# Gated linear attention and a low-rank mixer: two more units loaded raw and turned by VectorE, and another order in the first batch's attention

## The chip, the core and the metric

The kernel runs on one core of a Trainium2 chip. The metric is device microseconds of one execution. The four runs of the kernel before took 502.76 to 505.43 us, with a median of 503.75 us.

## What is computed

All inputs are random. There are 4 batches, 8 heads, 768 steps and 48 channels a head. The mixer works on 384 channels (8 heads of 48), with a rank of 32 and a hidden width of 1536.

```python
f = 1.0 / (1.0 + np.exp(-f_logit))
for t in range(S):                                  # attention, for each batch and head
    state = f[:, :, t, :, None] * state + np.einsum('bhd,bhe->bhde', k[:, :, t], v[:, :, t])
    y[:, :, t] = np.einsum('bhd,bhde->bhe', q[:, :, t], state)
x = y.transpose(0, 2, 1, 3).reshape(B, S, H * D)    # bridge
u = x + (x.transpose(0, 2, 1) @ U @ V).transpose(0, 2, 1)
out = u + np.maximum(u @ w_ch1, 0.0) @ w_ch2        # mixer
```

q, k, v and f_logit are 32-bit floats. The four weights U, V, w_ch1 and w_ch2 come as 64-bit floats, so the kernel makes 32-bit floats of them out of integer operations.

## The kernel before

**Units.** The attention is cut into 16 units: unit n is a pair of heads of batch n // 4. A unit's 768 steps are cut into 12 chunks of 64. In each unit, cumulative products of the gates f are made by scans; the keys k are multiplied by X (the product from a step to its chunk's end) and the queries q by Y (the product from the chunk's start). Then products of 48 or 64 rows give the scores inside a chunk (`sc`), what each chunk adds to the state (`ds`), and the output y out of both.

**Turning the inputs.** f, k and q have to stand with channels on the partitions. There are two ways. For batches 0 and 1 (`b < TURNED`, with TURNED = 2, so units 0 to 7) a tensor is loaded with steps on the partitions (line 394, two DMAs of 128x6x48), and TensorE turns it by six 128x128 transposes into PSUM (`on_tensor`, line 506). ScalarE (f, line 527) or VectorE (k and q, line 518) then read it from PSUM. For batches 2 and 3 (units 8 to 15) it is loaded in blocks of 32 steps (line 400, four DMAs of 32x24x32 or 32x24x16), and VectorE turns every 32x32 block (`turned`, line 483); the multiplication (line 521) then reads SBUF alone.

**The pieces of a unit.** The front of unit n has five: `gates` (f to the sigmoid `fz`), `keep` (scan X, and small operations on it, lines 540 to 550), `keys` (k times X, into `kz`), `read_back` (scan Y, line 558) and `queries` (q times Y, into `qT`). Each tensor's load for unit n + 2 is issued when unit n has read its buffer (`follow`, line 497). The rear has six: `kept` (TensorE turns kz back, line 610, and ScalarE copies it to `kb`, line 614), `states` (ScalarE's copy `whole`, line 618; the products `ds`, line 626; ScalarE's copy `added`, line 632), `scan` (VectorE, line 641, in place in `added`; for batches 1 to 3 ScalarE then copies the result to `st`, line 648), `scores` (line 589, then VectorE's mask A, line 596), `read` (products of q with the state, line 661, and ScalarE's small copy `seen`, line 668) and `inner` (products of A with v, line 679, then ScalarE's copy into the mixer's x, line 685).

**The mixer of a batch.** `low_rank` (line 146), `added_up` (line 154) and `mix` (line 171, with VectorE's addition to x, line 161), then `turn` (line 181), the first channel product `pz` (line 193, with ScalarE's relu, line 200) and the second: plain `po` (line 215) for batch 0, and a form with seven quarter products `pw` (line 238) for the others.

**What sets the order.** TensorE's order is written out by hand for the whole kernel, and so is that of VectorE and ScalarE for the part described here; behind that a scheduler orders VectorE and ScalarE. TensorE, VectorE, ScalarE and the DMA queue of SP each work in order. The stages are:

1. The attention of batch 0 alone, units 0 to 3 (lines 755 to 775). `busy(n)` puts n idle products (128x384, line 753) into TensorE's queue, whose result nobody reads.
2. The start of batch 0's mixer (from line 778), with one idle product ahead of each of its first three pieces, and one weight conversion (lines 64 to 69, on ScalarE, VectorE and GpSimd) put beside each piece but the second and third. From the tenth piece on (EARLY = 9), pieces of batch 1's attention are laid between.
3. The second product of batch 0, laid between the pieces of units 4 to 8 (line 796).
4. Batches 1, 2 and 3 in the same manner, without weight conversions.

**Buffers.** There are two sets of f, k and q buffers, used by even and odd units. In PSUM, a ring of three double banks (`ps_big`) serves pt, sc, ds, y, pu and put, and a ring of two banks (`ps_mm`) serves ph, pz, po and pw. `whole` and `kb` have one buffer each.

## Time and profile before

| | |
|---|---|
| median of 4 runs | 503.75 us (502.76 to 505.43) |
| the profiled execution | 503.66 us, of which the profile's span is 501.9 us |
| busy: TensorE, weight loads | 486.0 us, 405.2 us |
| busy: VectorE, ScalarE, GpSimd | 274.9 us, 157.4 us, 37.6 us |
| transposes of f, k, q on TensorE (line 506) | 144, of which 36 are those of units 6 and 7 |
| transposes on VectorE (line 483) | 24, of 128x768 each |
| idle products (line 753) | 17 (34 records) |
| DMA | 149269 packets, 34.32 MB |

"PE" is TensorE, "PEld" its weight loads, "DVE" VectorE, "ACT" ScalarE, "POOL" GpSimd, and "SPq" the DMA queue of SP. An ordinary 32-bit product leaves two records on PE, so "x6" of `po` is three products; a transpose leaves one. In timeline rows the first number is the start in us, the second the duration, and brackets hold the idle time of that engine ahead of it and what ended it.

### The profile page before, as it was taken

The page shows a single profiled execution, that of the slowest core. Times are in us where ns is not written, and L with a number is a line of the kernel's source. Part 1 is how long each engine was busy: PE and PEld are TensorE (multiplying, and loading weights), DVE is VectorE, ACT ScalarE, POOL GpSimd, SP SyncE. Part 2 cuts the span into 40 slices and gives each one's busy share as a digit, 9 for nine tenths or more (in the row PEclk, how much of TensorE's full clock was granted, in tenths as well). Part 3 has the DMA queues.
Part 4 walks back from the last instruction along what each step waited for, and adds up shares of the span by engine and source line. Part 5 has one row for each costly group of instructions (what it writes and reads, how often), then busy time and mean ns, then how long its engine had stood idle before and what let it go on. Part 6 is the DMA issues. An engine that isn't in the chain of part 4 may idle for free.

```text
span 501.9 us, 12045 instructions
## 1 busy us (share of the span) xinstructions
PE 486.0 (97%) x5319; PEld 405.2 (81%) x5319; DVE 274.9 (55%) x396; ACT 157.4 (31%) x297; POOL 37.6 (7%) x49
## 2 busy tenths in 40 slices
PE   6898999999999999999999999999999999999995
PEld 4666688887666568898898888898899888999995
DVE  5885989777587757656864436632411431222232
ACT  2424665564433313423332222413311122101010
POOL 3001345442000000000000000000000000000000
PEclk9997999999999999999999999999999999999999
DMA  9989977634667422424534100100000000000001
GB/s 145 152 171 230 205 190 173 174 88 62 105 106 112 81 40 29 66 28 88 64 50 80 25 31 3 25 1 34 2 3 31 2 33 1 0 33 0 33 1 39
DMA packets 149269, 34.32 MB, mean 68 GB/s; under 512 B 139798, under 2 KB 147670, under 8 KB 149206
## 3 DMA queue, kind: packets, MB, share of 16 engines
q1 hardware_dynamic: 149206, 33.44, 35.8%
q8 instruction: 44, 0.72, 0.6%
q14 instruction: 19, 0.16, 0.1%
HBM read 28.70 MB, written 4.72 MB: 67 GB/s over the span
## 4 chain that ended last, share of the span: by engine, by line
PE 92%; SPq 3%; DMA 3%; issue 1%; DVE 1%; ACT 0%
PE pz L193 38%; PE pw L238 25%; PE po L215 10%; PE pt L506 3%; PE y L661 3%; PE sc L589 3%; SPq L394 2%; PE y L679 2%; PE ds L626 2%; PE put L181 2%; DMA k_raw<-in_k_dram 1%; PE pt L610 1%; DMA f_raw<-in_f_logit_dram 1%; PE idle L753 1%; PE pu L171 1%; PE ph L146 1%
## 5 line engine op out<-in xcount | busy, mean ns | idle before, releaser
L193 PE MATMUL pz<-uT,w 128*128 128x256 f32 x864 | 195.8, 382 | 0.1
L193 PEld LDWEIGHTS pz<-uT,w 128*128 128x128 f32 x864 | 161.1, 190 | 22.1 <-issue 0.3
L200 ACT ACTIVATE z<-pz 128x512 f32<-128x512 f32 x63 | 37.6, 596 | 131.6 <-PE pz L193 127.5
L238 PE MATMUL pw<-w,z 128*128 128x192 f32 x324 | 56.5, 329 | 0.4 <-DVE o L161 0.4
L238 PE MATMUL pw<-zw,w_raw 128*128 128x192 f32 x324 | 55.9, 327 | 0.0
L238 PEld LDWEIGHTS pw<-w,z 128*128 128x128 f32 x324 | 52.8, 190 | 2.3 <-DVE o L161 1.6
L238 PEld LDWEIGHTS pw<-zw,w_raw 128*128 128x128 f32 x324 | 53.0, 190 | 1.3 <-DVE o L161 1.2
L161 DVE TENSOR_TENSOR w_raw<-z 128x768 f32<-128x768 f32 x18 | 17.2, 954 | 56.3 <-ACT z L200 56.3
L69 POOL TENSOR_TENSOR w<-w_y,w_r 128x384 int32<-128x384 int32 x24 | 31.5, 1311 | 35.9 <-DVE w_y L68 28.0
L540 DVE TENSOR_TENSOR_SCAN X<-fz,ends 128x768 f32<-128x768 f32 x16 | 28.1, 1756 | 10.7 <-ACT fz L527 6.4
L558 DVE TENSOR_TENSOR_SCAN Y<-fz,starts 128x768 f32<-128x768 f32 x16 | 27.9, 1745 | 0.2
L641 DVE TENSOR_TENSOR_SCAN added<-added,whole 128x576 f32<-128x576 f32 x16 | 21.6, 1352 | 9.0 <-ACT added L632 9.0
L215 PE MATMUL po<-w,zw 128*128 128x384 f32 x72 | 25.6, 499 | 0.0
L215 PE MATMUL po<-w,z 128*128 128x384 f32 x72 | 25.3, 495 | 0.0
L161 DVE TENSOR_TENSOR w_y<-x,pw 128x192 f32<-128x192 f32 x9 | 3.2, 354 | 38.5 <-ACT w_y L251 38.5
L596 DVE TENSOR_TENSOR A<-sc,causal 128x768 f32<-128x768 f32 x16 | 15.2, 947 | 16.1 <-PE sc L589 16.1
L648 ACT COPY st<-added 128x576 f32<-128x576 f32 x12 | 14.7, 1223 | 18.9 <-DVE added L641 18.9
L161 DVE TENSOR_TENSOR w_y<-w_y,pw 128x192 f32<-128x192 f32 x18 | 6.2, 347 | 25.6 <-PE pw L238 25.6
L215 PEld LDWEIGHTS po<-w,zw 128*128 128x128 f32 x72 | 12.9, 189 | 8.7 <-issue 1.2
L614 ACT COPY kb<-pt 128x768 f32<-128x768 f32 x16 | 12.8, 798 | 22.4 <-PE pt L610 22.4
L66 DVE TENSOR_SCALAR w_y<-w_y 128x384 f32<-128x384 f32 (+3 forms) x27 | 13.1, 485 | 11.8 <-ACT w_y L64 11.5
L215 PEld LDWEIGHTS po<-w,z 128*128 128x128 f32 x72 | 12.9, 190 | 8.1 <-DVE o L161 0.6
(102 smaller groups left out, 533.0 us busy)
## 6 DMA issues: line engine op xcount, KB each, us to landing
w_raw<-in_moe_w_ch_dram SPq DMA_DIRECT2D x18, 384.0 KB, 3.7
out_dram<-o SPq DMA_DIRECT2D x24, 192.0 KB, 1.9
f_raw<-in_f_logit_dram SPq DMA_DIRECT2D x16, 144.0 KB, 4.5
k_raw<-in_k_dram SPq DMA_DIRECT2D x16, 144.0 KB, 4.1
q_raw<-in_q_dram SPq DMA_DIRECT2D x16, 144.0 KB, 4.2
v_nat<-in_v_dram SPq DMA_DIRECT2D x16, 144.0 KB, 4.4
v_nat<-in_v_dram SPq DMA_DIRECT2D x32, 72.0 KB, 3.0
zw<-in_moe_w_ch_dram SPq DMA_DIRECT2D x6, 384.0 KB, 7.2
```

Source lines behind the costliest of these rows:

```text
L69: nc.gpsimd.tensor_tensor(dst.bitcast(I32), shaped(y.bitcast(I32)), shaped(r), ALU.add)
L161: nc.vector.tensor_tensor(*args)
L193: nc.tensor.matmul(pm[:, i * 2 * P : (i + 1) * 2 * P], lhsT=w1[:, m, o : o + P], rhs=uT[a][:, m, :], start=(m == 0), stop=(m == NDC - 1))
L200: nc.scalar.activation(z[a, c][:, k : k + 2, :].rearrange("p i t -> p (i t)"), pm, AF.Relu)
L215: nc.tensor.matmul(pm, lhsT=z[a, i // NI][:, i % NI, s * P : (s + 1) * P], rhs=w2[:, i, :], start=(i == 0), stop=(i == NFC - 1))
L238: nc.tensor.matmul(pm[:, n * HM : (n + 1) * HM], lhsT=lhs[:, i, :], rhs=rhs[:, i, :], start=(i == 0), stop=(i == NI - 1))
L506: nc.tensor.transpose(pt[:, 2 * c // NBL, c % (NBL // 2) * P : (c % (NBL // 2) + 1) * P], nat[n % 2][nm][:, c].rearrange("p h d -> p (h d) ...
L540: nc.vector.tensor_tensor_scan(backwards(X, S - 1, S), backwards(f, S, S), backwards(ends, S - 1, S), 0.0, ALU.mult, ALU.add,)
L558: nc.vector.tensor_tensor_scan(Y, f[:, 0:S], starts, 0.0, ALU.mult, ALU.add)
L589: nc.tensor.matmul(sc[part[s ^ par], par, c * C : (c + 1) * C], lhsT=T["k"][rows[par], chunk[2 * c + s]], rhs=T["q"][rows[par], chunk[2 * ...
L596: nc.vector.tensor_tensor(T["A"], sc[:, :, 0 : NBL * C].rearrange("p h (c i) -> p h c i", i=C), causal.unsqueeze(1).unsqueeze(1).broadcast ...
L641: nc.vector.tensor_tensor_scan(states, states, T["whole"].rearrange("p e c -> p (e c)"), 0.0, ALU.add, ALU.mult)
```

## The change

- `TURNED` becomes 6 and is compared with the unit, not the batch. Units 6 and 7 are therefore loaded in blocks of 32 and turned by VectorE, as units 8 to 15 are.
- ScalarE's copy `whole` moves from the beginning of `states` to `kept`, ahead of the copy `kb`, for all units.
- The scan of batch 0 writes to a tile of its own (`st`, two buffers) in the layout that it had in `added`. For the other batches the result is the same as before.
- Idle products: one in place of two at the beginning, and none ahead of the mixer's first piece.
- Unit 3 has its `states` ahead of the `read` of unit 2. Its own `read` comes ahead of the first two weight conversions, not after them.
- In batch 0's mixer no weight conversion is put beside the first piece; the one that was there stands beside the third piece.

```diff
-    TURNED = 2
+    TURNED = HP + HP // 2
...
-                if nm == "v" or b < TURNED:
+                if nm == "v" or n < TURNED:
...
         def operand(nm, of):
             t = T[nm] = kz[n % 2][:, C:] if nm == "k" else two.tile([P, S], F32, name="qT")
-            if b < TURNED:
+            if n < TURNED:
                 nc.vector.tensor_tensor(halves(t), on_tensor(nm), halves(T[of]), ALU.mult)
             else:
                 turned(t, r[nm])
...
         def gates():
             f0 = T["f0"] = two.tile([P, NCH], F32, name="f0")
-            if b < TURNED:
+            if n < TURNED:
...
+            whole = T["whole"] = one.tile([P, D, NCH], F32, name="whole")
+            nc.scalar.copy(whole, wholes[n % 2].unsqueeze(1).broadcast_to((P, D, NCH)))
             kb = T["kb"] = one.tile([P, 2, NBL, PAD], F32, name="kb")
             nc.scalar.copy(kb.rearrange("p h c d -> p h (c d)"), pt[:, :, 0 : NBL * PAD])
 
         def states():
-            whole = T["whole"] = one.tile([P, D, NCH], F32, name="whole")
-            nc.scalar.copy(whole, wholes[n % 2].unsqueeze(1).broadcast_to((P, D, NCH)))
...
         def scan():
 
-            states = added[:, 0 : D * NCH]
+            st = T["st"] = two.tile([P, NCH, D], F32, name="st")
+            by_e = "p (e c) -> p c e"
+            if b == 0:
+                states = st.rearrange("p c e -> p (c e)")
+                T["st"] = states.rearrange(by_e, c=NCH)
+            else:
+                states = added[:, 0 : D * NCH]
             with tc.high_priority(offset=AHEAD):
                 nc.vector.tensor_tensor_scan(
-                    states, states, T["whole"].rearrange("p e c -> p (e c)"), 0.0, ALU.add, ALU.mult
+                    states, added[:, 0 : D * NCH], T["whole"].rearrange("p e c -> p (e c)"), 0.0, ALU.add, ALU.mult
                 )
-                T["st"] = states.rearrange("p (e c) -> p c e", c=NCH)
                 if b > 0:
 
-                    st = two.tile([P, NCH, D], F32, name="st")
-                    nc.scalar.copy(st, T["st"])
-                    T["st"] = st
+                    nc.scalar.copy(st, states.rearrange(by_e, c=NCH))
...
-        busy(2)
+        busy(1)
...
-                pieces += rear(n - 1, "read") + rear(n, "states", "scan", "scores") + rear(n - 1, "inner")
+                pieces += rear(n, "states") + rear(n - 1, "read") + rear(n, "scan", "scores") + rear(n - 1, "inner")
...
-        for piece in loads[:2] + rear(HP - 1, "read", "inner") + loads[2 : early + 2]:
+        for piece in rear(HP - 1, "read") + loads[:2] + rear(HP - 1, "inner") + loads[2 : early + 2]:
...
-        idles = {0: 1, 1: 1, 2: 1}
+        idles = {1: 1, 2: 1}
...
-            if loads and i not in (1, 2):
+            if loads and i > 1:
                 loads.pop(0)()
```

## The prediction, made before the changed kernel ran

> **What bounds the kernel now.** I read the page's first two parts, then busy times by stretch, then the timelines of TensorE and VectorE in the stretches that the change touches.

> ```profile
> PE 486.0 (97%) x5319; PEld 405.2 (81%) x5319; DVE 274.9 (55%) x396; ACT 157.4 (31%) x297; POOL 37.6 (7%) x49
> ...
> PEclk9997999999999999999999999999999999999999
> ```

> TensorE is busy for all but 16 us, and its clock is below full in the fourth slice alone (37.6 to 50.2 us). By stretch (length, then busy time of PE, PEld, DVE, ACT, POOL, then clock, DMA share, GB/s):

> ```profile
> 39.80:43.20 3.40, 1.77 (x112) 1.63 (x104) 1.38 (x2) 1.37 (x3) 0.00 (x0) 1.00 1.15 318
> 43.20:46.60 3.40, 2.58 (x103) 2.42 (x96) 1.93 (x5) 1.63 (x6) 0.00 (x0) 0.52 0.83 151
> 46.60:50.10 3.50, 3.50 (x54) 2.01 (x58) 1.99 (x7) 1.95 (x5) 1.19 (x3) 0.50 1.04 166
> ...
> 113.00:140.00 27.00, 27.00 (x455) 18.47 (x457) 17.64 (x22) 10.65 (x20) 3.31 (x2) 1.00 0.59 85
> 140.00:168.00 28.00, 28.00 (x447) 17.50 (x440) 23.29 (x28) 10.84 (x20) 0.00 (x0) 1.00 0.66 104
> ```

> From 57.9 us, where the first `pz` starts, to about 496 us the same table shows less than half a microsecond of idle TensorE. There every microsecond off TensorE shortens the run, if nothing else becomes late. Ahead of 57.9 us the kernel is a chain of waits through DMA, TensorE, ScalarE and VectorE. The two halves are summed apart.

> **Units 6 and 7: what leaves TensorE.** TensorE's timeline where unit 6 is turned (f, then k):

> ```profile
> 112.72 0.82 PE L506 MATMUL pt<-ident,f_raw 128*128 128x128 f32 x6
> 113.38 2.10 PE L215 MATMUL po<-w,z 128*128 128x384 f32 x6
> 115.32 0.82 PE L506 MATMUL pt<-ident,k_raw 128*128 128x128 f32 x6
> 116.06 0.90 PE L661 MATMUL y<-st,qT 48*64 48x48 f32 x44
> ```

> The next group starts 0.66 us after f's six transposes and 0.74 after k's. The durations (0.82, or 0.27 each) overlap, so the pitch from start to start counts. The six groups that go hold 0.66, 0.74, 0.75, 0.71, 0.65 and 0.75: 4.26 us. A `po` group takes 1.94 us ahead of transposes and 2.13 ahead of the small products that now follow some of them. Laying the stretch from 112.72 to 140.36 out again with these pitches gives 23.85 us in place of 27.64: **3.8 us** off TensorE.

> **What VectorE gets.** It keeps the multiplications (0.95 us from PSUM, 0.96 from SBUF) and gets six transposes of 0.97, 5.8 us. VectorE does this already for units 8 and 9:

> ```profile
> 141.37 0.97 DVE L483 STREAM_TRANSPOSE fT<-f_raw 128x768 f32<-128x768 f32 x1
> 143.24 1.76 DVE L540 TENSOR_TENSOR_SCAN X<-fz,ends 128x768 f32<-128x768 f32 x1 [0.90 <-ACT fz L535]
> ...
> 153.46 0.97 DVE L483 STREAM_TRANSPOSE fT<-f_raw 128x768 f32<-128x768 f32 x1
> ```

> One unit takes it 12.1 us, from one fT to the next, including 0.9 us of waiting for ScalarE's sigmoid. TensorE's unit will take 23.85 / 2 = 11.9. So VectorE isn't free cover here: it is level with TensorE, and what counts is its lead. I followed its queue from the last weight conversion (ends at 115.3) with these durations, on the clock of before. kz of unit 6 is ready at 121.4 and TensorE comes to `kept` at 124.4; A of unit 5 is ready at 127.1, wanted at 129.6 (`ds` of unit 6 takes that bank of the ring); kz of unit 7 at 133.9, wanted at 136.5; scores' A of unit 6 at 140.2, wanted at 141.7. None is late. What is late is ScalarE: with six tiles fewer in the ring of three, `kept` of units 6 and 7 takes the bank that its copy of y into x frees, and that copy is queued behind `st`, which waits for VectorE's scan. It ends at 124.7 and 137.2, 0.3 and 0.4 us late (the second with the first counted). GpSimd's last conversion stretches a small VectorE operation at 117.05 to 0.79 us, where the same takes 0.17 at 130.40; a transpose there may lose as much. I take **0.9 us** of waits (0 to 2.5).

> The loads of these units change too: 24 DMAs in place of 12. Four issues hold SP for 2.04 us at 113.61, two for 0.97 at 88.06, so SP gets 6 x 1.07 = 6.4 us more; it is waiting for free weight buffers for 30.5 us in all. The packets double, by 9216. At the page's mean (35.8% of 16 x 501.9 us over 149206 packets, 19 ns) that is 11 us of all engines, where the stretch from 57.9 to 113 leaves 18.7 us of them unused. The weight loads queued behind are wanted four conversions later, some 11 us, and land in 3.7. Zero, with 1 us as the upper end if they slip.

> [...]

> **The start up to 37 us.** One idle product fewer lets f of unit 0 be turned up to 0.64 us earlier (its first weight load is at 4.82, after a wait for issue alone, the transposes at 5.46). That gain ends here:

> ```profile
> 19.92 0.85 PE L506 MATMUL pt<-ident,f_raw 128*128 128x128 f32 x6 [1.13 <-DMA f_raw<-in_f_logit_dram]
> ```

> Unit 2's f lands at 19.79, SP having issued without a pause since 0.8 us. Zero; even a slower start has 1.1 us of slack. From there to 37 us the order of TensorE and VectorE stays. `whole` goes from behind x to ahead of kb, in time in which ScalarE waits for TensorE, and has to wait for the scan of the unit before (17.9 us for unit 1's): kb comes up to 0.7 us later and is wanted 4 us later. Zero. In the later batches the copy is equally covered: ScalarE is 14 to 40% busy.

> **The start from 37 to 58 us.** `ds` of unit 3 ahead of `read` of unit 2 brings its scan forward by 0.8 us, but TensorE then halts for instructions (1.63 us at 40.93 before, ending at 42.56), which ends the scores of unit 3 at 43.2 in both. `seen` of unit 3 no longer stands behind four conversion operations (at 46.09, while `read` ended at 45.73): 0.35 us. The idle product ahead of `low_rank` goes: up to 0.8 us, but h stands behind conversions on ScalarE (51.37 before) and profits by 0.1 to 1.0. The largest piece is on VectorE:

> ```profile
> 54.55 0.56 DVE L68 SCALAR_TENSOR_TENSOR w_y<-zw,w_y 128x384 uint32<-128x384 uint32 x1
> 55.03 2.68 DVE L161 TENSOR_TENSOR x<-x,pu 128x768 f32<-128x768 f32 x3
> ```

> x waits behind the third w1 conversion (53.08 to 55.03), as h's second copy does on ScalarE. Both now go ahead of it. Following the chain (`ph`, h, `ph`, h, `pu`, x, `put`, uT, `pz`), `pz` starts at 56.55 with the clock at half as before and at 55.7 with it full: 1.3 to 2.2 us. The conversion moved is wanted at the second set of `pz`, 7.8 us after the first; it ends by about 59. I take **1.6 us** (-1.2 to 2.2).

> The lower end is the clock. Idle products are there to be busy, and three stretches above show what a gap costs: TensorE busy for 52% of 3.4 us, then 6.7 us at half speed. [...] By the row, a gap of 1.63 us sufficed. If half speed lasts one such stretch longer (to 53.5), the chain loses about 2.8 us against my sum, hence -1.2.

> **The sum.** 503.66 us (span 501.9 and 1.76 around it) - 3.8 + 0.9 - 1.6 = 499.16, so **499.2 us**. The profiled execution is 0.1 us below the median of 503.75.

> **Rivals.**
> - *The start gives nothing, or loses.* The clock stays at half longer, as above, and only the transposes count: 503.66 - 2.9 + 0.5 = 501.3. For it: fewer idle products and waits for h. Against it: the halt in unit 3's scores gets shorter, as `ds` now fills part of it. 16%.
> - *VectorE becomes the bound of units 6 and 7*, without a fall of the clock: waits of 2.5 us in place of 0.9, 500.8. For it: 12.1 us a unit against 11.9. 12%.
> - *Slower: waits for VectorE bring the clock down.* If VectorE or the copy behind it comes 1.3 us later than I have it, `kept` of units 6 and 7 waits 1.6 us each, the gap that sufficed before. Each then costs 1.6 and half of 6.7: 5.0. Two cost 9.9, and the time is 503.66 - 3.8 - 1.6 + 9.9 = 508.2. Against it: at units 8 and 9, with the same 12.1 us, TensorE never waits. 9%.
> - *The start gains more.* The shorter halt leaves the clock at full and `pz` starts at 55.7 or before; VectorE is in time: 503.66 - 3.8 - 2.2 = 497.7. 15%.

> The forecast itself has 48%, from 498 to 500.8.

> A measurement of this kernel can tell about 0.5% from no change, 2.5 us, so "faster" is below 501.2. The forecast and the fuller gain lie there, the second rival for the most part, and the first in a third: 0.76. Within 0.5%: 0.14. Slower: 0.10. The range goes from 497.0 (the fuller gain and some of the start's 20 us) to 502.2 (the first rival with its clock).

> **What will show it.** Line 483 with 30 transposes, the turning on TensorE with 108. First `pz` at 56.3 us or so, not 57.9. The distance from the first `pz` to the last product shorter by about 2.9. No TensorE wait over 0.6 us between 105 and 165. A granted clock of full from 58 us on. Unit 2's f still waited for at 19.8. I am wrong if `kept` waits for ScalarE's x by over a microsecond, if half speed shows behind 53 us or in units 6 and 7, or if a weight comes late to `po`.

## The result and the profile after

| | before | after |
|---|---|---|
| median | 503.49 us (501.53 to 506.36) | 502.1 us (499.88 to 505.27) |
| ratio after / before | | 0.9975, 95% interval 0.9966 to 0.9985 |
| profiled execution (span) | 503.66 us (501.9) | 502.02 us (500.3) |
| first `pz` starts | 57.89 us | 59.07 us |
| first `pz` to the last group of `pw` | 436.33 us | 433.43 us |

The change gains 0.25%, about 1.3 us, where 4.5 were forecast. The last two rows split it: behind the first `pz` the kernel is 2.9 us shorter, ahead of it 1.2 us longer. The page after, busy times and clock:

```profile
PE 482.3 (96%) x5279; PEld 401.2 (80%) x5279; DVE 279.2 (56%) x402; ACT 157.8 (32%) x297; POOL 36.3 (7%) x49
...
PEclk9997899999999999999999999999999999999998
```

TensorE has 3.7 us less to do. The same stretches as before, and one more (columns as there; the clock stands third from the end):

```profile
39.80:43.20 3.40, 0.62 (x31) 0.48 (x28) 1.36 (x1) 0.16 (x1) 0.00 (x0) 1.00 1.08 291
43.20:46.60 3.40, 3.15 (x127) 2.99 (x126) 0.96 (x1) 1.01 (x4) 0.00 (x0) 0.58 0.86 165
46.60:50.10 3.50, 2.42 (x56) 1.82 (x58) 2.50 (x9) 2.22 (x9) 1.04 (x2) 0.50 0.89 169
50.10:53.90 3.80, 3.80 (x15) 1.52 (x8) 3.40 (x7) 1.94 (x5) 1.56 (x3) 0.50 1.13 170
113.00:140.00 27.00, 27.00 (x459) 17.42 (x458) 23.69 (x32) 11.98 (x22) 2.02 (x3) 1.00 0.60 85
140.00:168.00 28.00, 28.00 (x413) 16.82 (x412) 24.73 (x30) 10.62 (x21) 0.00 (x0) 1.00 0.79 123
```

TensorE works for 0.62 us of the first stretch, where it worked for 1.77 before. It is at half speed from 43.8 to 54.0, where it was from 43.3 to 50.1. Between 113 and 168 us it has no idle time, although VectorE is now busy for 88% of it.

**Units 6 and 7.** TensorE's timeline at unit 6's front and at its `kept`:

```profile
114.03 2.10 PE L215 MATMUL po<-w,z 128*128 128x384 f32 x6
116.06 0.90 PE L664 MATMUL y<-st,qT 48*64 48x48 f32 x44
...
124.31 1.45 PE L215 MATMUL po<-w,zw 128*128 128x384 f32 x4
125.70 0.59 PE L610 MATMUL pt<-ident,kz 64*128 64x64 f32 x12
```

No transposes of f and k stand around the `po` group, and `kept` shows no wait. ScalarE's copy of y into x, whose bank it takes, ran from 125.01 to 125.65: it was in time, by 0.05 us. From the first `pz` to the first one of batch 1's mixer it took 127.6 us before and takes 123.8: 3.8 us less.

**The start.** TensorE's timeline before, then after ("issue" is a wait for which the profile shows no releaser):

```profile
42.56 0.74 PE L589 MATMUL sc<-qT,kz 48*64 48x64 f32 x35 [1.63 <-issue]
...
48.00 1.65 PE L753 MATMUL idle<-ends,ident 128*128 128x384 f32 x2
49.58 1.74 PE L146 MATMUL ph<-x,U 128*32 128x384 f32 x12
51.25 0.91 PE L753 MATMUL idle<-ends,ident 128*128 128x384 f32 x2
```

```profile
39.82 0.47 PE L589 MATMUL sc<-qT,kz 48*64 48x64 f32 x11
43.07 0.74 PE L589 MATMUL sc<-qT,kz 48*64 48x64 f32 x34 [2.78 <-issue]
43.59 1.40 PE L682 MATMUL y<-v_nat,A 64*64 64x48 f32 x48
...
49.40 2.77 PE L146 MATMUL ph<-x,U 128*32 128x384 f32 x12 [0.84 <-POOL V L69]
52.10 1.65 PE L756 MATMUL idle<-ends,ident 128*128 128x384 f32 x2
...
59.07 1.10 PE L193 MATMUL pz<-uT,w 128*128 128x256 f32 x4
```

The halt in unit 3's scores, 1.63 us before, is 2.78. It ends at 43.07, where it ended at 42.56. `ph` starts at 49.40, where it started at 49.58: up to here the change is still 0.18 us ahead, since the idle product ahead of `ph` is gone. What it loses, it loses behind it, at half speed: `ph` (1.74 us before) takes 2.77 and the idle product behind it 1.65 (0.91 before).

**A new wait where batch 2's mixer begins.** TensorE, then ScalarE, after:

```profile
279.25 1.48 PE L146 MATMUL ph<-x,U 128*32 128x384 f32 x12
281.52 2.71 PE L238 MATMUL pw<-zw,w_raw 128*128 128x192 f32 x15 [0.79 <-DVE o L161]
```

```profile
279.65 0.83 ACT L535 ACTIVATE fz<-fT 128x756 f32<-128x756 f32 x1 [3.73 <-DVE fT L483]
280.39 0.30 ACT L251 COPY w_y<-pw 128x192 f32<-128x192 f32 x1
```

Before, this place had no wait. The copy of `pw` to w_y can go as soon as `pw` ends at 279.3, but stands behind a sigmoid that waits for VectorE's turn of f. The scheduler now puts that turn behind four additions for `w_raw` (before: behind one), a reordering far behind the edit. VectorE before, then after:

```profile
277.61 0.96 DVE L161 TENSOR_TENSOR w_raw<-z 128x768 f32<-128x768 f32 x1 [3.89 <-ACT z L200]
278.49 0.97 DVE L483 STREAM_TRANSPOSE fT<-f_raw 128x768 f32<-128x768 f32 x1
...
277.77 0.95 DVE L161 TENSOR_TENSOR w_raw<-z,w_raw 128x768 f32<-128x768 f32 x1
278.64 0.97 DVE L483 STREAM_TRANSPOSE fT<-f_raw 128x768 f32<-128x768 f32 x1
```

### The profile page after: what moved, and what is told of

It reads as the page before. It is cut to its first block, busy times and chain, and to the rows that moved or that the text cites. A ratio compares the mean times of both kernels' runs of the same rounds, so it can differ in the third digit from the quotient of the medians.

```text
span 500.3 us, 11989 instructions
## 1 busy us (share of the span) xinstructions
PE 482.3 (96%) x5279; PEld 401.2 (80%) x5279; DVE 279.2 (56%) x402; ACT 157.8 (32%) x297; POOL 36.3 (7%) x49
## 2 busy tenths in 40 slices
DMA packets 158676, 34.30 MB, mean 69 GB/s; under 512 B 149206, under 2 KB 157078, under 8 KB 158614
## 3 DMA queue, kind: packets, MB, share of 16 engines
q1 hardware_dynamic: 158614, 33.44, 36.3%
## 4 chain that ended last, share of the span: by engine, by line
PE 92%; DVE 2%; DMA 2%; SPq 2%; issue 1%; ACT 1%; POOL 0%; DVEq 0%; POOLq 0%; ACTq 0%
PE pz L193 38%; PE pw L238 24%; PE po L215 10%; PE y L664 3%; PE sc L589 3%; PE y L682 2%; PE ds L626 2%; PE pt L506 2%; PE put L181 2%; PE pt L610 1%; PE idle L756 1%; SPq L394 1%; PE ph L146 1%; PE pu L171 1%; DMA f_raw<-in_f_logit_dram 1%
## 5 line engine op out<-in xcount | busy, mean ns | idle before, releaser
L200 ACT ACTIVATE z<-pz 128x512 f32<-128x512 f32 x63 | 37.6, 596 | 129.9 <-PE pz L193 125.8
L161 DVE TENSOR_TENSOR w_raw<-z 128x768 f32<-128x768 f32 x18 | 17.2, 954 | 56.3 <-ACT z L200 56.3
L540 DVE TENSOR_TENSOR_SCAN X<-fz,ends 128x768 f32<-128x768 f32 x16 | 28.1, 1757 | 10.0 <-ACT fz L535 5.1
L69 POOL TENSOR_TENSOR w<-w_y,w_r 128x384 int32<-128x384 int32 x24 | 30.2, 1257 | 36.8 <-DVE w_y L68 32.7
L215 PE MATMUL po<-w,zw 128*128 128x384 f32 x72 | 25.6, 499 | 0.0
L215 PE MATMUL po<-w,z 128*128 128x384 f32 x72 | 25.3, 496 | 0.0
L161 DVE TENSOR_TENSOR w_y<-x,pw 128x192 f32<-128x192 f32 x9 | 3.2, 354 | 38.2 <-ACT w_y L251 38.2
L161 DVE TENSOR_TENSOR w_y<-w_y,pw 128x192 f32<-128x192 f32 x18 | 6.3, 349 | 25.5 <-PE pw L238 25.5
L215 PEld LDWEIGHTS po<-w,zw 128*128 128x128 f32 x72 | 12.9, 189 | 8.7 <-issue 1.2
L215 PEld LDWEIGHTS po<-w,z 128*128 128x128 f32 x72 | 13.1, 190 | 8.5 <-DVE o L161 0.6
L238 PE MATMUL pw<-w,w_raw 128*128 128x192 f32 x108 | 19.2, 328 | 0.0
L682 PEld LDWEIGHTS y<-v_nat,A 64*64 64x64 f32 x768 | 14.0, 144 | 6.1 <-issue 4.8
L238 PEld LDWEIGHTS pw<-w,w_raw 128*128 128x128 f32 x108 | 17.7, 190 | 1.1 <-issue 1.1
```

What stands on the lines that cost most here:

```text
L69: nc.gpsimd.tensor_tensor(dst.bitcast(I32), shaped(y.bitcast(I32)), shaped(r), ALU.add)
L161: nc.vector.tensor_tensor(*args)
L200: nc.scalar.activation(z[a, c][:, k : k + 2, :].rearrange("p i t -> p (i t)"), pm, AF.Relu)
L215: nc.tensor.matmul(pm, lhsT=z[a, i // NI][:, i % NI, s * P : (s + 1) * P], rhs=w2[:, i, :], start=(i == 0), stop=(i == NFC - 1))
L238: nc.tensor.matmul(pm[:, n * HM : (n + 1) * HM], lhsT=lhs[:, i, :], rhs=rhs[:, i, :], start=(i == 0), stop=(i == NI - 1))
L540: nc.vector.tensor_tensor_scan(backwards(X, S - 1, S), backwards(f, S, S), backwards(ends, S - 1, S), 0.0, ALU.mult, ALU.add,)
```

## The experiments

The theory: the transposes give all that was forecast of them, and the start loses it again, because TensorE halts longer for its instructions and its clock stays at half for longer. The rivals: VectorE is late for units 6 and 7 after all; the start loses by its missing idle products, or by the moved conversion. The table's comparisons are with the kernel before on the same chip; single profiles differ among themselves, and where they speak against the medians, the medians count.

| kernel | median us | ratio to before, 95% interval |
|---|---|---|
| e1 transposes alone | 500.21 | 0.9934 [0.9912, 0.9957] |
| e2 start alone | 506.01 | 1.0040 [1.0027, 1.0053] |
| e3 change, idle products back | 501.85 | 0.9955 [0.9938, 0.9971] |
| e4 change, four w1 loads later | 500.75 | 0.9941 [0.9922, 0.9961] |
| e5 transposes, conversion | 500.04 | 0.9934 [0.9915, 0.9953] |
| e6 transposes, order | 502.97 | 0.9978 [0.9962, 0.9995] |
| e7 transposes, fewer idle products | 501.48 | 0.9957 [0.9937, 0.9977] |
| e8 transposes, four w1 loads later | 502.99 | 0.9987 [0.9968, 1.0006] |
| e9 transposes, copy on VectorE | 500.53 | 0.9934 [0.9911, 0.9956] |
| e10 transposes of units 4 and 5 too | 509.86 | 1.0114 [1.0083, 1.0145] |
| e12 transposes, states first | 501.90 | 0.9964 [0.9944, 0.9983] |
| e13 transposes, read first | 500.97 | 0.9941 [0.9921, 0.9961] |
| e14 transposes, conversion, fewer idle products | 500.77 | 0.9944 [0.9923, 0.9965] |
| e15 transposes, order, fewer idle products | 502.41 | 0.9967 [0.9945, 0.9989] |
| e16 e5 with the copy on VectorE | 499.40 | 0.9919 [0.9888, 0.9949] |
| e17 e5 with two w1 loads later | 500.42 | 0.9936 [0.9914, 0.9958] |
| e18 change, six w1 loads later | 505.24 | 1.0028 [1.0008, 1.0048] |
| e19 e5 with four w1 loads later | 499.19 | 0.9907 [0.9886, 0.9927] |

**e1 and e2: each half alone.** e1 is the kernel before with this edit; e2 is the change without it.

```diff
-    TURNED = 2
+    TURNED = HP + HP // 2
...
-            if b < TURNED:
+            if n < TURNED:
```

> The kernel before with units 6 and 7 loaded raw and turned by VectorE, and nothing else of the change. Theory (the transposes give what TensorE's pitches say, and the start takes it back): from the first pz to the end 3.9 us less, so 499.6 us, ratio 0.992; if the scheduler's order of the sigmoid ahead of the copy of pw in batch 2 comes along with it, 0.8 us less of that, 500.4. Rival (the transposes give little, because the stage stands on VectorE or the DMA): 502 us or more, ratio 0.997 or above.

> The changed kernel with units 6 and 7 turned by TensorE as before: all of the change but the transposes. Theory: slower than the kernel before by what the start loses, 1.2 us in the two profiles, 504.7 us, ratio 1.002 to 1.005, and a mean clock below 0.99. Rival (transposes give little): the start is then what makes the change 1.3 us faster, 502.2 us, ratio 0.9975.

The transposes alone gain 3.4 us (500.21 beside 503.64), the start alone loses 2.4 by the medians and 2.0 by the ratio, more than the 1.2 between the two profiles. The sum of both is close to the whole change. e1's page and its timeline at the start:

```profile
PEclk9999999999999999999999999999999999999998
```

```profile
41.87 0.74 PE L589 MATMUL sc<-qT,kz 48*64 48x64 f32 x35 [1.34 <-issue]
...
47.62 1.48 PE L146 MATMUL ph<-x,U 128*32 128x384 f32 x12
```

In this execution the clock never fell before the very end, with a halt of 1.34 us. e1's start is that of before, edit for edit, whose profile has two stretches at half speed. So one profile doesn't tell what a start is worth; the medians do. The batch-2 wait of 0.8 us is in e1 and not in e2: it comes with the transposes.

**e3: the change with its idle products back.**

```diff
-        busy(1)
+        busy(2)
...
-        idles = {1: 1, 2: 1}
+        idles = {0: 1, 1: 1, 2: 1}
```

> The changed kernel with the two idle products back (two at the beginning, one ahead of low_rank). Theory (an idle product fewer leaves TensorE at half speed for one stretch of 3.4 us more): half speed ends at about 50 us, not 53.7, the first pz starts 1.5 us earlier, 500.6 us, ratio 0.994. Rival (the new order of pieces lengthens the halt for instructions and is the cause by itself): half speed lasts as long, 502 us, ratio 0.9975.

501.85 beside 502.1 us. By the ratios 1.0 us is theirs, with an error of as much, and the intervals overlap: the rival has it, or nearly.

**e5, e6, e7, e14, e15: the start's three parts.** e5 moves the conversion, e6 has the new order with all that belongs to it (the copies, `st`), e7 takes two idle products away, all from e1. e14 and e15 combine them.

```diff
-            if loads and i not in (1, 2):                 # e5, e14
+            if loads and i > 1:
...
-        busy(2)                                           # e7, e14, e15
+        busy(1)
...
-        idles = {0: 1, 1: 1, 2: 1}
+        idles = {1: 1, 2: 1}
...
-                pieces += rear(n - 1, "read") + rear(n, "states", "scan", "scores") + rear(n - 1, "inner")
+                pieces += rear(n, "states") + rear(n - 1, "read") + rear(n, "scan", "scores") + rear(n - 1, "inner")   # e6, e15
...
-        for piece in loads[:2] + rear(HP - 1, "read", "inner") + loads[2 : early + 2]:
+        for piece in rear(HP - 1, "read") + loads[:2] + rear(HP - 1, "inner") + loads[2 : early + 2]:
```

> On the transposes alone: the weight conversion beside the mixer's first piece is left out, as in the change. All three edits of the start together have cost 2.0 us (the start alone gave 506.0 us beside 503.6), so each of the three is tried by itself on top of the transposes, which alone gave 500.2 us. If the loss is one of instruction fetches and of TensorE's clock, the conversion, which lies on ScalarE, VectorE and GpSimd, does nothing for it: 500.2 us within 0.6, first hidden-layer product at 56.6 us within 0.5. If the loss is that work is late for those engines, the conversion left out gains about 1 us (499.2).

> On the transposes alone: the other order of unit 3 and the copies (states ahead of unit 2's read, unit 3's read ahead of the conversions, scan into st of batch 0); the idle products and the conversions stay as they were before. This is the start's change minus its two other parts. If the order costs it (the idle products of unit 3 no longer lie where the queue halts for instructions, so that the halt falls into unit 3's scores behind the six weight loads), it loses 1 to 2 us against the 500.2 us of the transposes alone: 501.2 to 502.2, with a halt of over 2 us in unit 3's scores and a first hidden-layer product at 58 to 59 us. If the idle products alone cost it, 500.2 us within 0.6 and a halt of 1.6 or less. As forecast at first: 498.6 us, first hidden-layer product at 55.0.

> On the transposes alone: two idle products fewer (one at the very start, one ahead of the mixer's first piece), everything else as before. With the whole change these two put back gave 501.85 us instead of 502.1, so little is expected of them: if the clock of the mixer's beginning needs the product that filled 48.0 to 49.6 us, TensorE stays at half speed for one more stretch of 3.4 us and loses 1.0 to 1.7 us (501.2 to 501.9); if they only take time, 500.2 us less 0.4 (499.8).

> The transposes with the conversion moved and the two idle products fewer, the order as before. If the order carries the loss, this is as the transposes alone: 500.0 to 500.8 us. If the idle products carry it (as 501.5 us for them alone suggests), 501.3 to 502.0.

> The transposes with the new order and the two idle products fewer, the conversion as before. If the order carries the loss by itself, 502.0 to 503.0 us, with or without the idle products. If order and idle products each cost something that adds up, 503.5 to 504.5. If fewer idle products make up for the order, 500.5 to 501.5.

With e1, e3 and the change itself these are all eight combinations. Averaged over the four pairs of each part, from the ratios and with about 0.7 us of error each: the order costs 1.3 us (0.9969 with it, 0.9942 without), the idle products 0.5 (0.9961, 0.9950), the conversion -0.35 (0.9952, 0.9959). Only the first is clear of its error.

What these parts do to the clock shows better in the mean clock that the record gives for every execution. The clock that an execution lost, (1 - mean clock) times its span, averages 6.2 us over the change's 44 executions, and 3.5 us over the 135 of the kernel before that ran beside the experiments. Over the same eight combinations, the new order loses 1.6 us of clock and the missing idle products 2.0, each with an error of 0.7; the conversion loses nothing (-0.2). So the idle products do keep the clock up, as they are there to do; but they take time themselves (0.91 us each at full speed and 1.65 at half in the rows of `idle` above), and little is left of it in the medians.

e6's timeline has the halt that was expected if the order costs it:

```profile
43.36 0.74 PE L589 MATMUL sc<-qT,kz 48*64 48x64 f32 x35 [3.04 <-issue]
```

**e12 and e13: the order's two parts**, each from e1. In e12 unit 2's `read` takes what unit 3's `states` have just written to `added`, not unit 2's states, so unit 2's y is another one. The order and the amount of work are those meant, but that `read` now waits for ScalarE's copy `added`, 0.82 us in the profile, a wait that the change does not have.

```diff
+                pieces += rear(n, "states") + rear(n - 1, "read") + rear(n, "scan", "scores") + rear(n - 1, "inner")   # e12
...
+        for piece in rear(HP - 1, "read") + loads[:2] + rear(HP - 1, "inner") + loads[2 : early + 2]:                # e13
```

> On the transposes alone: only one part of the new order, unit 3's states ahead of unit 2's read. The whole new order made 502.97 us of 500.1. If it is this part that moves the instruction fetch behind the loads (packet at 40.4 to 41.5 us in the four profiles with the new order, at 39.3 to 40.0 in the four with the old), the halt in unit 3's scores is 2.5 us or more and the time 501.7 to 503. If it is the other part, 500.2 within 0.6 and a halt of 1.1 to 1.8 us.

> On the transposes alone: only the other part of the new order, ScalarE's copy after unit 3's read ahead of the first two weight conversions. TensorE's own order stays as it is. If unit 3's last products wait for instructions and not for ScalarE (they begin 2.3 to 2.9 us after an instruction packet in every profile, whatever they are put down to), this changes nothing: 500.2 us within 0.6. If they wait for the copy, which now comes about 1.2 us earlier, it gains 0.5 to 1 us (499.4). If the conversions of U and V, now later by one copy, hold up the mixer, it loses up to 0.5 (500.7).

Read as four cells with e1 and e6, the states ahead of `read` cost 1.7 us (0.0033), the `read` ahead of the conversions 0.55 (0.0011), each with an error of 1.0. e12's extra wait is part of the 1.7; between e13 and e6, which have no such wait, it is 1.9 us (0.0037), with an error of 1.3. Yet e12's own profile has a halt of 1.73 us, and e13's one of 3.26, though its TensorE stream is e1's. My expectation that the packet's place tells one order from the other fell with that: e13's packet came at 41.2 us.

**e4, e8, e17, e18, e19: the w1 loads.** Six loads of 384 KB are begun at 32 us, ahead of unit 5's. Here four (e4 on the change; e8 on e1; e19 on e5), two (e17 on e5) or all six (e18 on the change) are begun after unit 5's loads.

```diff
-    for start, _ in loads[:n]:
+    for start, _ in loads[begun:n]:
...
-                loads = ahead_by(early + FIRST, weights)
+                for begin, _ in weights[: early + 2]:     # + 4 in e17, + 0 in e18
+                    begin()
...
+            if n == 3:
+                loads = ahead_by(early + FIRST, weights, early + 2)
```

> The changed kernel with four of the six early w1 loads issued after the loads of units 4 and 5 instead of ahead of them. Theory (TensorE's halt at 40 us is its instructions waiting behind 2.3 MB of w1 on the DMA engines): the halt shrinks from 2.8 us to under 1, the clock stays at full, the first pz starts before 57.5 us, and the time is 499 to 500.5 us, ratio 0.992. Rival (the instructions are asked for late, whatever the DMA does): the halt stays at 1.5 us or more, half speed too, and the time is that of the changed kernel, 502, or above it where weights come late.

> On the transposes alone: four of the six w1 loads that begin at 33 us are begun after the loads of unit 5 instead (as in the earlier trial on the whole change, which went from 502.1 to 500.75 us). If it is those loads that hold up the instructions at 40 to 45 us, the halt in unit 3's scores falls from 1.34 us to under 0.9 and the time by 0.5 to 1.0 us: 499.2 to 499.7. If the trial on the whole change gained only by luck of the clock, 500.2 us within 0.5. If w1 comes too late for its conversions, slower than 501.

> The transposes with the conversion moved, and two of the six early w1 loads (not four) begun after the loads of unit 5. With four, the halt fell to 1.1 us but the third w1 load landed 2 us late for its conversion, and the time was 503.0. If that lateness was the loss, two gives the shorter halt without it: 499.3 to 499.8 us. If the loads have little to do with the halts, 500.0 within 0.5. If loads begun behind unit 5's are late here too, 501 or more.

> The whole change, with all six early w1 loads (not four) begun after the loads of unit 5. If the instruction packet stands behind those loads, it comes at 38 us or before and the halt in unit 3's scores is at most the 0.89 us that four later left of 2.78; w1 then lands late for the first hidden-layer products, which wait for it, and the time is 502 us or more for that reason. If the packet's place has little to do with the loads, the halt is again between 1.7 and 3.2 us.

> The transposes with the conversion moved and the old order, and four of the six w1 loads later: against the whole change with the same four later (500.75 us) it differs by order and idle products alone. If the order costs its 1.3 us only because its halt lies behind the loads, the two are alike: 500.75 within 0.7, both with a halt of about 1 us in unit 3's scores. If the order costs it in another way too, 499.4. If the loads begun later are themselves what loses (503.0 in the trial that kept the conversion in its old place), 502 or more.

The DMA view of the profile after, 40.3 to 40.5 us, shows what TensorE's halt waits behind:

```profile
q1 hardware_dynamic: 75, 0.07, 109.3%
q8 instruction: 1, 0.02, 35.0%
```

One instruction packet, 16 KB, in a time in which the loads fill all 16 engines. That it is TensorE's, and that the halt waits for it, shows when TensorE's records are counted. The page after has 43 packets on this queue and 10558 records (products and weight loads), one packet to 246. And here is what TensorE had done at 42 us, in the middle of the halt, before and after:

```profile
0.00:42.00 42.00, 34.52 (x724) 25.54 (x725) 31.22 (x40) 15.12 (x31) 4.66 (x22) 1.00 1.06 175
0.00:42.00 42.00, 33.77 (x724) 25.02 (x725) 32.06 (x40) 15.72 (x31) 4.66 (x22) 1.00 1.06 178
```

1449 records with either order, although the change has one idle product fewer ahead of it and other products. In all 20 profiles the halts of over 0.2 us put down to "issue" between 20 and 50 us stand behind 689, 1196, 1449 and 1703 or 1704 records, and nowhere else: multiples of 253 to 255 apart. They belong to the count, not to the piece of the program. With the halts and the clock of the same profiles:

| | w1 loads at 32 us | instruction packets at, us | second one after record 1196 | halt in unit 3's scores | half speed, us | first `pz` |
|---|---|---|---|---|---|---|
| before | 6 | 32.9, 40.0, 43.8 | 4.1 | 1.63, ends 42.56 | 6.8 | 57.89 |
| after | 6 | 33.2, 40.4, 44.4 | 4.7 | 2.78, ends 43.07 | 10.2 | 59.07 |
| e1 | 6 | 32.9, 39.5, 43.0 | 4.1 | 1.34, ends 41.87 | 0 | 56.59 |
| e6 | 6 | 32.7, 40.7, 44.8 | 5.6 | 3.04, ends 43.36 | 6.8 | 58.99 |
| e13 | 6 | 33.2, 41.2, 44.9 | 5.7 | 3.26, ends 43.82 | 10.2 | 59.82 |
| e17 | 4 | 33.1, 39.1, 43.8 | 3.3 | 1.06, ends 41.98 | 3.4 | 57.27 |
| e4 | 2 | 32.5, 38.6, 43.5 | 2.7 | 0.89, ends 41.46 | 3.4 | 56.97 |
| e8 | 2 | 32.6, 38.6, 43.4 | 3.0 | 1.09, ends 41.72 | 3.4 | 59.48 |
| e19 | 2 | 33.1, 37.5, 41.7 | 2.1 | none | 0 | 55.69 |
| e18 | 0 | 33.0, 38.3, 42.3 | 2.6 | 0.43, ends 41.02 | 6.8 | 61.01 |

The second packet is taken 3.5 to 5.7 us after TensorE passed record 1196 in the fifteen profiles with six loads, and 2.1 to 3.3 us after it in the five with fewer; the third, behind the loads, 1.1 to 2.1 us after record 1449 in all twenty. TensorE goes on 2.3 to 3.5 us after a packet, in every profile with a halt. On the change itself the halt is 2.78, 0.89 and 0.43 us with six, two and no loads there: this is shown as far as the loads go. Where six loads stay, the halt averages 1.8 us over nine profiles with the old order (1.07 to 3.26) and 2.7 over five with the new (2.20 to 3.18; e12, with one of its two parts, 1.73). A shorter halt isn't always due to the loads: e17's 1.06 us is that of e5, which has all six at 32 us (1.07), and its 500.42 us is what was expected if the loads have little to do with it. e19's timeline, the old order and two loads:

```profile
40.02 0.88 PE L589 MATMUL sc<-qT,kz 48*64 48x64 f32 x42
...
47.56 0.91 PE L753 MATMUL idle<-ends,ident 128*128 128x384 f32 x2
```

The scores run through, and the idle product takes 0.91 us rather than 1.65. e19 is the fastest of all, 4.3 us ahead of before. Of the three outcomes expected the second came: with the same later loads the new order (or the fewer idle products) costs in another way too, or e4 would be as fast. But that the halt is gone in this one profile is not the order's doing: e8 has the same loads and the same TensorE order, and halts for 1.09 us.

That a halt is gone isn't enough, though. In e8 ScalarE comes to its third w1 conversion before that load has landed, and h stands behind it:

```profile
53.01 0.55 ACT L64 ACTIVATE w_y<-zw 128x384 f32<-128x384 f32 x1 [2.09 <-DMA zw<-in_moe_w_ch_dram]
53.46 0.54 ACT L65 ACTIVATE w_r<-zw 128x384 int32<-128x384 uint32 x1
53.90 0.46 ACT L156 COPY h<-ph 128x384 f32<-128x384 f32 x1
```

In e19, where the conversion is moved, h goes ahead of the same wait (50.03 us), and by the ratios 4.0 us lie between the two, about half of it TensorE's wait for h in e8 (1.98 us). So the moved conversion, worth nothing by itself, is what makes later loads possible. It is not free in e19 either: uT stands behind the conversion there, and the first `pz` waits 1.33 us for it. e18 pays with a wait of 3.66 us for h.

**e9 and e16: the copy of the new wait made by VectorE**, on e1 and on e5.

```diff
-                nc.scalar.copy(s[:, hi], pm[:, lo])
+                nc.vector.tensor_copy(s[:, hi], pm[:, lo])
```

> On the transposes alone: the copy of one product to w_y in the mixers of batches 1 to 3 is made by VectorE, where ScalarE made it (nine copies, 0.32 us each). If TensorE's new wait of 0.8 us in batch 2 comes from this copy standing behind a sigmoid on ScalarE, the wait goes, and the time falls by 0.5 to 0.8 us from the 500.2 us of the transposes alone: 499.4 to 499.7. If the wait is VectorE's own lateness (its queue is full there), the wait stays and the time is 500.2 within 0.5. If VectorE's nine copies get in the way elsewhere, slower than 500.7.

> The transposes with the conversion moved, and with VectorE making the copy to w_y, which took the wait of 0.8 us in batch 2 down to 0.2. The profile with the copy alone showed the wait gone, but its median (500.5) did not fall below that of the transposes (500.2). If the wait that went is a gain like any other, 499.4 to 499.7 us; if it is given back, 500.0 to 500.5.

In the profiles the wait is gone, and the distance from the first `pz` to the last `pw` group falls from 433.30 us (e1) to 432.52 (e9) and 432.67 (e16). The ratios say 0 and -0.8 us, both with an error of over 1 us. The cause of the wait is shown; its worth, 0.8 us, only by the profile.

**e10: units 4 and 5 turned by VectorE too** (`TURNED = HP`).

> On the transposes alone: units 4 and 5 too are loaded raw and turned by VectorE, so that 72 transposes leave TensorE instead of 36. By the same price as measured for units 6 and 7 (3.3 to 3.9 us for 36) this would be another 3.5 us: 496.7 us. If VectorE has no room at 60 to 110 us, where its row shows 80 to 85% with the weight conversions, its turns (0.97 us each, six of them) come late, TensorE waits, and the gain is lost: 500 us or more, with waits of TensorE for VectorE at 65 to 115 us. The middle case, half of it lost, is 498.5.

509.86 us: the bad case, and more than it. ScalarE's timeline:

```profile
97.38 0.83 ACT L535 ACTIVATE fz<-fT 128x756 f32<-128x756 f32 x1 [3.90 <-DVE fT L483]
98.12 0.21 ACT L536 ACTIVATE f<-fT 128x12 f32<-128x12 f32 x1
98.23 0.58 ACT L200 ACTIVATE zw<-pz 128x512 f32<-128x512 f32 x1
```

VectorE turns f late, behind two conversions; ScalarE's sigmoid waits for it for 3.9 us, and the relu that frees TensorE's bank stands behind the sigmoid. TensorE then waits 8.2 us for such relus between 69 and 111 us. Of the 11.5 us between this profile and e1's, 7.6 lie behind the first `pz`; the rest is lost ahead of it, where the halts are longer (1.23, 2.19 and 1.68 us). This is the rival "VectorE becomes the bound": wrong for units 6 and 7, right one stage earlier, and through ScalarE's queue.

## Why the prediction fell short

- **Transposes, -3.8 us: right.** -3.8 in the profile. The pitch rows held: VectorE has six turns of 0.97 us more to do (its busy time rises by 4.3 us), TensorE 3.8 less, and the time falls by 3.3 to 3.4 (e1).
- **Waits for VectorE and ScalarE at `kept`, +0.9 us: none came.** Counted from the first `pz`, TensorE came to unit 6's `kept` when I had it (66.6 us; forecast 66.5), but the copy of y was done earlier: at 66.6 (66.8), and for unit 7 at 78.6 (79.3). In its stead a wait of 0.8 us came in batch 2, which I hadn't looked for: I took the order of the later batches as given. First `pz` to last product was to be 2.9 us shorter, and is 2.90: luck, since two errors cancel. The loads of these units were rightly put at zero, but for a wrong price: the 9408 packets more cost 1.9 us of all engines (36.3% of the span beside 35.8%), not 11.
- **Start up to 37 us, zero: right.** Unit 2's f is still waited for, 0.99 us at 19.86.
- **Start from 37 to 58 us, -1.6 us: this step failed.** It measured +1.2 in the profile, and about +2.0 by e2's ratio. First `pz` was to start at 56.3 us and starts at 59.07: 2.8 us, which is nearly the whole error (499.16 forecast, 502.02 in the profiled execution). The step said that the halt "ends the scores of unit 3 at 43.2 in both", and took half speed "as before". The halt came out 1.15 us longer, and half speed lasted a stretch longer, as the first rival had it; what decided was the half speed, since `ph` still started 0.18 us earlier than before. I had named this very case, "half speed lasts one such stretch longer", and its price, "about 2.8 us". Against that rival I held that "the halt in unit 3's scores gets shorter, as `ds` now fills part of it". It is the other way round: `ds` and unit 2's `read` were both already ahead of the halt and only change places, so nothing new fills it. It ends behind an instruction packet that comes through the loads (2.6 us after the one at 40.0 before, 2.7 after the one at 40.4 in the change), not a fixed time after TensorE arrives. From record 1196 to 1449 TensorE worked for 4.57 us, where it worked for 4.99 (with an idle product fewer ahead, one less falls between these counts), and the packet came 0.59 us later behind record 1196: hence most of the 1.15.
- **The idle products:** by the row of the profile before (a halt of 1.63 us, then 6.8 us at half speed) their going was a risk, and the row was right. In the clock's windows (see the last section) TensorE was busy for all of 46.7 to 50.1 us before, with the idle product at 48.00, and full speed came back. After, it was busy for 2.57 us of 47.2 to 50.6, and half speed stayed:

```profile
46.72:50.13 3.41, 3.41 (x54) 1.89 (x57) 1.92 (x7) 1.95 (x5) 1.17 (x3) 0.50 1.04 164
47.19:50.60 3.41, 2.57 (x55) 1.65 (x56) 2.50 (x10) 2.09 (x6) 1.21 (x3) 0.50 0.86 161
```

- **VectorE and ScalarE in that stretch:** x no longer waits behind a conversion, as forecast, but waits 2.56 us for `pu`, which is late itself. The gain was off the chain that ended last.

What stays open is why the new order makes the packet later on average (4.9 us behind record 1196 over five profiles, 4.1 over nine with the old). TensorE comes to the place of the halt at 40.3 to 40.5 us with either order (after, e6, e1), and with the same TensorE stream the halt was 1.34 us in one profile and 3.26 in another. e4 and e19, with the same later loads, still differ by 0.0034 of before, 1.7 us with an error of 1.4. They differ in order and idle products, which these runs don't separate any further.

## What to carry over

The halts in unit 3's scores, which these profiles put down to "issue", ended 2.3 to 3.5 us after an instruction packet. So where such a gap shows, count the engine's records up to it, look up the instruction packets and what else is on the DMA at that time, before moving work around it. Taking two idle products away lost 2.0 us of clock here, so look at the clock's window where one lies before taking it away. Moving 36 transposes off the full engine gave 3.8 us in the profile, as their pitch said, where the receiving engine's queue, and every queue behind it, had a lead; the same step one stage earlier cost 9 us. Where several small edits ride on one large one, measure the large one alone: here it was the better kernel, 500.2 us against 502.1.
